# A two-layer attention and feed-forward kernel: the last 512 tokens in two halves of 256, with the closing work tile by tile

## Chip, cores, metric

One core of a Trainium2 chip. The metric is the device time of one execution in microseconds (us), as the median of several runs. A profile of one further execution gives the *span*, from the first to the last instruction; it lies 1.7 to 2.0 us under the time of that same execution.

## The reference, cut to what matters

```python
def _A_ref(x, wqkv, wo):          # 2048 tokens, width 512, 32 heads of 16
    qkv = (x @ wqkv) ...          # split into q, k, v by head
    scores = jnp.einsum("bhqd,bhkd->bhqk", q, k) * scale
    p = _softmax(scores, axis=-1)
    o = jnp.einsum("bhqk,bhkd->bhqd", p, v)
    return o.reshape(B, S, D) @ wo
def _B_ref(x, w1, b1, w2, b2):    # feed-forward, hidden width 1376
    h = _gelu(jnp.einsum("bsd,df->bsf", _layernorm(x), w1) + b1)
    return jnp.einsum("bsf,fd->bsd", h, w2) + b2

x = x + _A_ref(_layernorm(x), ...);  x = x + _B_ref(_layernorm(x), ...)
x = x + _A_ref(_layernorm(x), ...);  x = x + _B_ref(_layernorm(x), ...)
```

Every token attends to all 2048, so layers 1 and 3 (the attentions) each need 32 x 2048 x 2048 exponentials.

## The kernel before

The program is made by a list scheduler in Python: jobs hand it tasks with a modelled duration and a priority, and it fixes the order of instructions on each engine. That order is then the program; on the chip each engine runs its list and waits on semaphores. In modelled gaps of TensorE it puts *fillers*, multiplications by zeros that are meant to keep the clock up.

Attention goes block of 512 queries by block, and in each block head group by head group (8 groups of 4 heads). A *score tile* is 128 keys of one head by 512 queries. Four heads lie on four 32-row strips of TensorE, so tiles of different heads run at once. ScalarE exponentiates two or three tiles in one instruction; some tiles go to VectorE, which computes the exponential by a polynomial. Values are then accumulated in one PSUM bank, `ACCB`:

```python
ops.append(I(lambda e, ...: e.matmul(self.ps[:, b, :], lhsT=self.KT[32*hp:32*hp+32, hg, kb*128:(kb+1)*128],
             rhs=self.QT[32*hp:32*hp+32, q, :], start=True, stop=True, tile_position=(32*hp, 0)), ...))
yield Task("pe", 0.0, ops)
... e.activation(out=self.PT[:, pt:pt+n, :], in_=self.ps[:, b0:b0+n, :], func=ACTF.Exp, scale=EXPS)
```

When value matmuls are issued is decided in `try_pv`; the last line matters below:

```python
for it in near:                       # ready tiles of the current head group
    hp = sg["tiles"][it[1]][1]
    if hp not in seen:                # at most one tile for each strip
        seen.add(hp); pick.append(it)
        if len(pick) == 4: break
left = sg["n"] - sg["sub"]
if len(pick) < 4 and len(near) < min(left, 5):
    return                            # wait for more
```

At the end of a head group (`job_segend`) VectorE transposes the accumulator, divides and transposes back. When all 8 groups of a block are done, its projection, norm and feed-forward follow (`job_post`, `job_ffn`), beside the next block's scores. Those of the very last block have nothing beside them:

```python
def job_post(self, L, qc):
    yield ("keys", [("ot", L, qc, hg) for hg in range(8)])       # all head groups
    for i, tt in enumerate(tiles): ...                           # 4 projections, one after the other
    yield from self.ln_group(tiles, slot, ...)                   # statistics of all 4
    for i, tt in enumerate(tiles): S_.spawn(self.job_yt(...))    # scale, transpose by DMA
    yield ("keys", [("yt", L, tt) for tt in tiles])
    S_.spawn(self.job_ffn_tail(L, qc) if tail else self.job_ffn(L, qc), pr)
```

## Time and profile before

| | us |
|---|---|
| time, median of 4 runs (range) | 1851.19 (1846.91 to 1852.32) |
| span in the profile | 1851.3 |
| ScalarE / TensorE / VectorE busy | 1737.9 / 1723.7 / 1590.1 |
| last exponential ends at | 1804.67 |
| tail after it | 46.63 |

TensorE's busy time includes 519 us of fillers, so it is not a bound. The prediction shows the main lines. One more view is needed, the waits that end ScalarE's idle time in the last block. I give the last block one measure throughout: **U**, from the start of the accumulator transpose that ends the 72nd head group (the last group of the block before; 1587.22) to the end of the last exponential. U is 217.45 us. The *waits* view of the kernel before over that window (engine and tile, what it waited for, us in total, times, longest):

```profile
ACT PT L973 <- PE ps L967: 5.7, 11, 0.8
```

Four of the 11 waits are of 0.80 to 0.82 us (a fifth, of 0.78, is only 0.55 and 0.49 in runs c and f, whose scores have the same order). This is one of the four, in the *timeline* (start, duration, engine, line, tiles, number; in brackets the idle time ahead and what ended it):

```profile
1700.28 1.26 PE L905 MATMUL ps<-wqkv,zw 128*128 128x256 bf16 x10
1701.47 0.51 PE L1099 MATMUL ps<-PT,V 128*17 128x512 bf16 x4
1701.92 0.60 PE L967 MATMUL ps<-QT,KT 32*128 32x512 bf16 x6
1702.38 2.37 ACT L973 ACTIVATE PT<-ps 128x1024 bf16<-128x1024 f32 x2 [0.82 <-PE ps L967]
```

Ten fillers (the scheduler had foreseen a hole), then four value matmuls, then six score tiles at once: two groups of scores stood behind a full probability buffer. ScalarE, the bound, had nothing to do for 0.82 us. That the buffer was full is read from the scheduler, not from the trace (see the experiments).

### The profile page before, as it was taken

Reading aid. Unit: us, or ns where it says so; the run is one execution under the profiler, and the core shown is the slowest. Engines: PE = TensorE matmul, PEld = TensorE weight load, DVE = VectorE, ACT = ScalarE, POOL = GpSimd, SP = SyncE. Lnnn points to the kernel's source line nnn. Section 1 sums busy time; section 2 is a strip of 40 time slices with the busy share of each in tenths; the row PEclk is TensorE's granted clock in tenths of the full one; section 3 lists DMA queues with packets and bytes.
Section 4 is the critical chain, followed back from the end, with each engine's and each line's share of the span. In section 5 each row is a group of like instructions: output and inputs, shape, how many; then the busy total and the mean of one; then the engine's idle time right before and its main releaser. Section 6 shows DMA issues by size and latency. Waiting matters only on the chain.

```text
span 1851.3 us, 32298 instructions
## 1 busy us (share of the span) xinstructions
PE 1723.7 (93%) x13057; PEld 664.7 (36%) x13057; DVE 1590.1 (86%) x2469; ACT 1737.9 (94%) x1539; POOL 171.1 (9%) x324
## 2 busy tenths in 40 slices
PE   6989899999999999999999999999999999999997
PEld 2223333333333333333333333333333333333344
DVE  6789999988898999979987999878899789987972
ACT  4989999999999999999999999999999999999991
POOL 4122221100100110002000023100000000000000
PEclk9999999999999999999999999999999999999999
DMA  6551000100100200014310110000000000010001
GB/s 157 97 116 32 24 21 12 33 12 24 56 18 4 55 27 7 15 27 101 50 31 7 29 44 21 15 12 13 7 7 18 15 7 7 7 15 15 1 1 24
DMA packets 147226, 54.80 MB, mean 30 GB/s; under 512 B 131879, under 2 KB 140936, under 8 KB 147080
## 3 DMA queue, kind: packets, MB, share of 16 engines
q1 hardware_dynamic: 147080, 52.72, 12.8%
q8 instruction: 107, 1.75, 0.4%
q14 instruction: 39, 0.32, 0.1%
HBM read 8.69 MB, written 15.30 MB: 13 GB/s over the span
## 4 chain that ended last, share of the span: by engine, by line
ACT 53%; PE 36%; DVE 6%; DMA 2%; issue 1%; POOL 1%; SPq 0%; POOLq 0%; DVEq 0%
ACT PT L973 50%; PE ps L967 11%; PE ps L1099 7%; PE ps L905 5%; PE ps L1216 4%; PE ps L742 4%; PE ps L1250 3%; PE ps L1184 3%; ACT h L1243 2%; DMA xnT<-xn 1%; DVE dt L984 1%; DMA yT<-xn 1%; DVE de L1054 1%; DVE de L1051 1%; ACT L973 0%
## 5 line engine op out<-in xcount | busy, mean ns | idle before, releaser
L973 ACT ACTIVATE PT<-ps 128x1024 bf16<-128x1024 f32 (+1 forms) x1466 | 1665.0, 1289 | 59.8 <-PE ps L967 55.7
L967 PE MATMUL ps<-QT,KT 32*128 32x512 bf16 x4096 | 599.9, 382 | 85.8 <-ACT PT L973 61.3
L905 PE MATMUL ps<-wqkv,zw 128*128 128x256 bf16 x3508 | 518.8, 275 | 0.0
L1099 PE MATMUL ps<-PT,V 128*17 128x512 bf16 x3633 | 436.5, 384 | 3.6 <-DVE accT L1127 3.2
L984 DVE TENSOR_SCALAR dt<-ps 128x512 int32<-128x512 f32 x463 | 317.5, 686 | 136.1 <-PE ps L967 132.9
L905 PEld LDWEIGHTS ps<-wqkv,zw 128*128 128x128 bf16 x3508 | 289.7, 98 | 208.2 <-issue 176.2
L967 PEld LDWEIGHTS ps<-QT,KT 32*128 32x128 bf16 x4096 | 163.8, 91 | 499.5 <-issue 297.8
L1051 DVE SCALAR_TENSOR_TENSOR de<-dt 128x1024 bf16<-128x1024 uint16 (+1 forms) x244 | 283.8, 1164 | 2.2
L1054 DVE SCALAR_TENSOR_TENSOR de<-dt,dv 128x1024 uint16<-128x1024 int32 (+1 forms) x244 | 283.0, 1161 | 1.9
L1099 PEld LDWEIGHTS ps<-PT,V 128*17 128x17 bf16 x3633 | 105.2, 87 | 240.0 <-issue 204.9
L1053 DVE TENSOR_TENSOR dv<-de,dv 128x1024 f16<-128x1024 bf16 (+1 forms) x244 | 160.3, 658 | 2.1
L1052 DVE TENSOR_SCALAR dv<-dt 128x1024 bf16<-128x1024 uint16 (+1 forms) x244 | 161.0, 661 | 0.0
L1099 PE MATMUL ps<-de,V 128*17 128x512 bf16 x463 | 138.8, 384 | 2.1 <-DVE accT L1127 1.2
L678 POOL TENSOR_SCALAR rs<-mv 128x4 f32<-128x4 f32 (+1 forms) x19 | 10.0, 527 | 1070.5 <-DVE mv L671 1070.2
L1216 PE MATMUL ps<-yT,w 128*128 128x512 bf16 (+1 forms) x352 | 98.3, 392 | 8.0 <-DMA yT<-xn 6.9
L742 PE MATMUL ps<-wqkv,xnT 128*128 128x512 bf16 x336 | 95.4, 391 | 8.8 <-DMA xnT<-xn 8.0
L1250 PE MATMUL ps<-w,h 128*128 128x512 bf16 x280 | 74.8, 382 | 0.6 <-DVE xres L1252 0.3
L1127 DVE STREAM_TRANSPOSE accT<-ps 128x512 f32<-128x512 f32 x80 | 57.0, 712 | 16.1 <-PE ps L1099 14.4
L1184 PE MATMUL ps<-wo,OT 128*128 128x512 bf16 x256 | 69.2, 382 | 0.2
L1236 DVE TENSOR_SCALAR h<-ps,b1c 128x512 f32<-128x512 f32 (+1 forms) x77 | 56.8, 737 | 6.3 <-PE ps L1216 5.9
L1099 PEld LDWEIGHTS ps<-de,V 128*17 128x17 bf16 x463 | 31.5, 87 | 40.0 <-issue 31.3
L1216 PEld LDWEIGHTS ps<-yT,w 128*128 128x128 bf16 (+1 forms) x352 | 27.6, 101 | 50.8 <-issue 25.7
(123 smaller groups left out, 773.9 us busy)
## 6 DMA issues: line engine op xcount, KB each, us to landing
q_scr<-qk SPq DMA_DIRECT2D x22, 256.0 KB, 2.0
k_scr<-qk SPq DMA_DIRECT2D x12, 256.0 KB, 2.0
q_scr<-h SPq DMA_DIRECT2D x10, 256.0 KB, 2.1
out_dram<-xres SPq DMA_DIRECT2D x16, 128.0 KB, 1.7
v_scr<-vst SPq DMA_DIRECT2D x12, 136.0 KB, 1.9
V<-v_scr SPq DMA_DIRECT2D x8, 204.0 KB, 5.0
wqkv<-in_A_wqkv_dram SPq DMA_DIRECT2D x3, 512.0 KB, 5.0
w<-in_B_w_dram SPq DMA_DIRECT2D x4, 344.0 KB, 5.3
```

The source lines that it names most:

```text
L742: yield Task("pe", prio, [I(lambda e, c=c: e.matmul(self.ps[:, b, :], lhsT=xnT[:, c, :], rhs=self.wqkv[:, c, which * 512:which * 512 + 512 ...
L905: P.op("pe", lambda e: e.matmul(self.ps[:, b, 0:w], lhsT=self.zw[:, :], rhs=rhs, start=st, stop=st, skip_group_check=True), [("zw",), R], ...
L967: ops.append(I(lambda e, hp=hp, hg=hg, kb=kb, q=q, b=b: e.matmul(self.ps[:, b, :], lhsT=self.KT[32 * hp:32 * hp + 32, hg, kb * 128:(kb + 1 ...
L973: S_.submit(Task("act", 1e-5 * gi, [I(lambda e, pt=pt, n=n, b0=b0: e.activation(out=self.PT[:, pt:pt + n, :], in_=self.ps[:, b0:b0 + n, :] ...
L984: S_.submit(Task("dve", 0.0, [I(lambda e, ds=ds, w=w: e.tensor_scalar(out=self.dt32[:, ds, w * 512:(w + 1) * 512], in0=self.ps[:, DLANE, : ...
L1051: yield Task("dve", pr(), [I(lambda e: e.scalar_tensor_tensor(out=E, in0=lo, scalar=65536.0, in1=lo, op0=ALU.subtract, op1=ALU.mult), RT, ...
L1052: yield Task("dve", pr(), [I(lambda e: e.tensor_scalar(out=v, in0=lo, scalar1=CUB_B * sc / 65536.0, scalar2=CUB_A * sc, op0=ALU.mult, op1= ...
L1053: yield Task("dve", pr(), [I(lambda e: e.tensor_tensor(out=D, in0=E, in1=v, op=ALU.mult), [("de", es), ("dv", s)], [("dv", s)], 0.12 + 0.5 ...
L1054: yield Task("dve", pr(), [I(lambda e: e.scalar_tensor_tensor(out=Pb, in0=t32, scalar=2.0 ** -9, in1=D, op0=ALU.mult, op1=ALU.subtract), R ...
L1099: ops.append(I(lambda e, hp=hp, hg=hg, kb=kb, ap=ap, first=first: e.matmul(self.ps[32 * hp:32 * hp + 17, ACCB, :], lhsT=self.V[:, hg, kb, ...
L1216: yield Task("pe", pr, [I(lambda e, c=c: e.matmul(self.ps[0:M, b, :], lhsT=self.w1[:, c, fc * 128:fc * 128 + M], rhs=self.yT[:, c, :], sta ...
L1250: yield Task("pe", pr, [I(lambda e, fc=fc, i=i, b=b: e.matmul(self.ps[:, b, :], lhsT=self.gt(fc, i), rhs=self.w2[:, fc, :], start=(fc == 0 ...
```

## The change

The intent: less work behind the last exponential. The last block becomes two blocks of 256 queries, so that only 256 tokens are left for the tail. A score tile of the half-width blocks holds two key blocks side by side, 512 columns again, so exponentials keep their shape. The tail's projection is accumulated head group by head group as they end, each tile has its own statistics, and TensorE transposes in place of the DMA. In the tail's feed-forward, a second-layer matmul now waits for the gelu of its own chunk of the hidden width, not for that of four chunks. Nothing else changes: the other blocks keep widths and modelled durations.

```diff
+        four = [tuple(range(4 * c, 4 * c + 4)) for c in range(self.NC)]
+        self.units = {1: four, 3: four[:3] + [four[3][:2], four[3][2:]]}
...
+            g = 512 // sg["W"]
+            sg["tiles"] = [(sg["kbs"][k:k + g], hp) for k in range(0, len(sg["kbs"]), g) for hp in range(4)]
...
+    def score(self, sg, j, b):
+        return [I(lambda e, ...: e.matmul(self.ps[:, b, i * W:(i + 1) * W], lhsT=self.KT[..., kb * 128:(kb + 1) * 128], rhs=self.QT[..., q, 0:W], ...)) for i, kb in enumerate(kbs)]
...   (value matmuls likewise; accumulator, transposes and scalings W wide)
-    def job_ffn_tail(self, L, qc):
+    def job_tail(self, L, qc):
+        yield ("keys", [("post",) + self.prev(L, qc)] + [("ot", L, qc, hg) for hg in range(7)])
+        for i, tt in enumerate(tiles):
+            S_.spawn(self.tail_tile(L, qc, tt, slot, i, left), 1.0 + 0.1 * i)
         yield ("keys", [("scores_done",)])
+        yield Task("act", pr, [... activation(out=self.kmx[:, 2:3], ..., func=ACTF.Gelu_apprx_tanh) ...])   # loads the table early
...   (feed-forward as before, W wide)
+    def tail_tile(self, L, qc, tt, slot, i, left):
+        pr = 0.9
+        b = yield ("get", "mb")
+        for h0 in range(8):
+            if h0 == 7:
+                yield ("keys", [("ot", L, qc, 7)])
+            yield Task("pe", pr, [... matmul(self.ps[:, b, :], lhsT=self.OT[:, h0, i*128:(i+1)*128], rhs=self.wo[:, h0, :], start=(h0 == 0), stop=(h0 == 7)) ...])
+        ...  # add, bn_stats, bn_aggr, variance and power on GpSimd, scale
+        yield Task("pe", pr, [... transpose(...) for k in range(4)])
+        yield Task("dve", pr, [... tensor_copy(out=self.yT[:, :, i*128:(i+1)*128], in_=...) ...])
```

## The prediction

> **What bounds the kernel now.** I read the page first: the sliced busy row of ScalarE (ACT) and the chain of waits.
>
> ```profile
> ACT  4989999999999999999999999999999999999991
> ...
> ACT 53%; PE 36%; DVE 6%; DMA 2%; issue 1%; POOL 1%; SPq 0%; POOLq 0%; DVEq 0%
> ACT PT L973 50%; PE ps L967 11%; PE ps L1099 7%; PE ps L905 5%; PE ps L1216 4%; PE ps L742 4%; PE ps L1250 3%; PE ps L1184 3%; ACT h L1243 2%; DMA xnT<-xn 1%; DVE dt L984 1%; DMA yT<-xn 1%; DVE de L1054 1%; DVE de L1051 1%; ACT L973 0%
> ```
>
> ScalarE is full from the third slice to the last but one, with the exponentials of L973 carrying half of the chain. Only the last slice (46 us) has it nearly empty. So there are two regimes: a long stretch where the time is ScalarE's, and a tail. The last exponential ends at 1804.67 in the timeline (1803.65 + 1.02), and the span is 1851.3, so the tail is 46.63 us. I cut the last 250 us into windows, two for the last 512 tokens' scores and two for the tail.
>
> ```profile
> core 0: us, PE busy (x) PEld busy (x) DVE busy (x) ACT busy (x) POOL busy (x), PEclk, DMA share, GB/s
> 1604.00:1704.00 100.00, 94.55 (x707) 35.99 (x707) 81.73 (x124) 95.56 (x81) 2.40 (x2) 1.00 0.08 16
> 1704.00:1804.67 100.67, 93.88 (x785) 40.33 (x783) 83.93 (x118) 99.05 (x88) 0.00 (x0) 1.00 0.00 1
> ...
> 1804.67:1825.37 20.70, 14.89 (x106) 9.75 (x104) 9.41 (x20) 1.28 (x2) 1.20 (x2) 0.97 0.15 27
> 1825.37:1851.30 25.93, 21.93 (x88) 9.06 (x88) 2.49 (x4) 7.55 (x11) 0.00 (x0) 0.89 0.06 21
> ```
>
> In the second window ScalarE idles 1.6 us of 100.67. The first also holds the projection, norm and feed-forward of the previous 512 tokens; ScalarE idles 4.4 us there. In the tail it works 8.84 us of 46.63. The chain says what the tail waits for:
>
> ```profile
> 1804.59 0.53 PE ps L1099 x5
> ...
> 1807.39 5.62 PE ps L1184 x26
> ...
> 1816.75 0.19 DVE mv L671
> ...
> 1818.78 2.45 DMA yT<-xn
> ...
> 1821.75 0.87 SPq L1209
> ...
> 1822.72 2.52 DMA yT<-xn
> ...
> 1825.37 7.60 PE ps L1216 x22
> 1832.97 4.32 PE ps L1282 x20
> 1837.29 3.45 PE ps L1216 x16
> 1840.74 3.45 PE ps L1282 x16
> ```
>
> Four 128-token tiles go through the projection one after another, all four are normalised, two rounds of transposing DMAs follow, and then come 88 matmuls of 512 columns. The first of those 88 are slow: 22 in 7.60 us, later 16 in 3.45 (0.216 each). Ahead of them TensorE had waited 5.81 us.
>
> **What the Trainium skill says.** "TensorE: Matmul & The Clock Gate", section "Back-to-back issue gap", gives N/2.4 + 2.5 ns warm: 216 ns at 512 columns and an estimate of 109 at 256. The trace agrees: 3.45/16 = 0.216, and the 128x256 fillers of L905 come 0.11 us apart. Its section "What's actually happening" says an idle window of some 3.4 us halves the clock; here 5.81 us of idling was followed by matmuls 0.43 us apart. "Part 3: Packing small matmuls", section "The mechanism", says that a weight load overlaps matmuls in flight only where the row group differs. That would hurt score tiles built from two matmuls on one row strip. The trace does not show the harm: a group of four scores took 0.40 us, and another, where I read two tiles on one strip, took 0.59, just one more pass of 512 columns. "ScalarE: Activation LUTs", section "What ACT_TABLE_LOAD costs", gives 1283 ns per load; all loads here take 1283.
>
> **The change, part by part.** (a) *The first half's feed-forward moves under the scores of the second half.* ScalarE is the bound there, so its gelu is paid in full: two table loads 2 x 1.283 = 2.57; the 5120-column gelu takes 4.471, and with 2560 columns fewer at 0.833 ns it is 2.34; the 512-column one of 0.631 becomes 0.42. With gaps 5.4 us. Its VectorE work takes score tiles away from VectorE:
>
> ```profile
> 1604.00:1704.00 100.00, 17.20 (x25) 1.00 0.08 16
> 1704.00:1804.67 100.67, 20.54 (x30) 1.00 0.00 1
> ```
>
> These are the VectorE score loads (L984) in the same two windows: 25 tiles beside a whole block's post-processing, 30 without. Half a block: 2.5 tiles, at 0.427 us of ScalarE each, 1.1 us. ScalarE's waits for scores were 4.0 against 1.6 us, so half of the difference, 1.2 us, comes as waiting.
>
> (b) *16 head-group ends instead of 8.* One end on VectorE is 0.712 + 0.246 + 0.420 + 0.699 = 2.08 us. VectorE's slope is 1.0 ns a column (1217 ns for 1024 columns, 700 for 512), so at half width 0.45 + 0.25 + 0.29 + 0.44 = 1.43. 16 x 1.43 - 8 x 2.08 = 6.3, plus about 1.5 for 8 more query scalings: 7.8 us. A VectorE score tile costs 0.686 + (1217 + 1215 + 688 + 683)/2 ns = 2.59 us, so 3.0 tiles go to ScalarE: 1.3 us. Beside the last 8 ends, once the post-processing is over, the timeline shows two ScalarE stalls of 0.82 us (at 1702 and 1737); 8 more ends, 1.6 us.
>
> (c) *Score and value matmuls of the unit double in number at half width.* Exponentials keep count and shape, since a 512-column tile now holds two key blocks. On TensorE the extra cost lies in slack. In 1704 to 1804.67 there are 245 score and 253 value matmuls; the fillers alone take 42.84 us. Even 25 ns for each of about 500 added matmuls is 12 us of that. Charge: 0.
>
> Sum for ScalarE: 5.4 + 1.1 + 1.2 + 1.3 + 1.6 = 10.6 us. The last exponential would end at 1815.3.
>
> (d) *The tail for 256 tokens*, counted from the last exponential, T. The end of the last head group starts 0.49 after T as now, 1.43 of work and 0.12 of gaps: T + 2.04. Seven of eight head groups are already accumulated for tile 0 and can be for tile 1, so 0.49 later (as now) its add starts, T + 2.53. Two adds and two statistics at about 0.66 (VectorE takes the other tile while one waits), then the aggregation 0.18: T + 5.4. GpSimd: 0.19 and then 0.583 for one column (four columns took 1.01), with 0.2 of gaps: T + 6.3. The second tile's power follows at T + 7.0, its scaling 0.42, four TensorE transposes about 0.4 with latency, a PSUM copy of 0.53 (the one such copy in the trace) with latency: first feed-forward matmul at about T + 8.6, against 20.70 now. The idle stretches of TensorE are short and filled, so I count it warm. Then 44 x 0.11 + 22 x 0.216 = 9.6 us of matmuls and 0.5 for the last gelu not covered: T + 18.7. The last two matmuls start 0.43 before that; 0.41 later the first add, two adds 1.29, the store 2.12 (1849.18 to 1851.30 now): T + 22.1. Now it is 46.63: 24.5 us less.
>
> Sum: 1851.3 + 10.6 - 24.5 = 1837.4 of span; the timed median lies 0.5 above the span, so about **1838 us**, 0.75% faster. Up to some 1590 us nothing changes: the other blocks keep their widths and modelled durations, hence their order.
>
> **Rivals.** *TensorE becomes the pace-setter of the last unit.* Each group of scores or values then has two passes with weight loads between; if each of the some 165 exponentials of those two windows waited 0.1 us more, 17 us would go and the time would be near 1855. For it: the skill's sentence on row groups, and that a wait for scores already ends most of ScalarE's idling. Against: the 0.59 us group above and the 42.84 us of fillers. *The tail starts cold.* If transposes and fillers do not keep the clock up, the 44 narrow matmuls take up to 0.213 each, 4.5 us more: about 1842. Against: clock 0.97 up to 1825.37, lost after idling of 5.8 us, which the new chain does not have in one piece. *The exposed work hides better than I charge*: if VectorE's added work falls in its idle 17% and no stalls come, only the 5.4 us remain and the time is 1833. *The tail is limited by chains between engines*: tile 1's steps may not interleave with tile 0's, and the order is fixed by a model of durations; 3 us either way.
>
> **Range and chances.** The cost side may be 6 to 18 us, the gain 20 to 26. Not all extremes meet, so 1830 to 1847. Faster by over 2% needs less than about 1815.5, that is 36 us; the tail cannot give that as 22 us of it must stay. Slower by over 2% needs some 60 us lost in a 210 us unit, only under the first rival at three times its size. So 0.02, 0.96 and 0.02.
>
> **What would show it.** In the changed kernel: the last exponential near 1815 (1810 says the hidden work was nearly free, over 1822 that TensorE or the ends hold ScalarE up); one gelu of 2.3 us with two table loads among the last unit's exponentials; the last unit's exponential count about 5 higher; ScalarE's waits for scores in the last 100 us near 4 us. After it: first feed-forward matmul 8 to 10 us after the last exponential, no transposing DMA there, matmuls 0.11 us apart, 22 to 24 us from last exponential to end. The prediction is wrong if score groups make ScalarE wait regularly, or if the tail keeps 30 us.

## More of the kernel before

(The execution profiled before took 1853.09 us, longer than the four timed.)

The probabilities have five buffers (three of three tiles, two of two), and a buffer comes free when all its tiles have been multiplied with the values.

## The result, and the profile after

| | before | after |
|---|---|---|
| time, median of 4 runs (range), us | 1851.19 (1846.91 to 1852.32) | 1829.3 (1827.47 to 1831.81) |
| span of the profile | 1851.3 | 1827.5 |
| U (last block up to the last exponential) | 217.45 | 219.34 |
| tail after the last exponential | 46.63 | 23.19 |

A ratio here is the mean time of one kernel's fast runs over that of the other's of the same rounds, so not quite the ratio of the medians: 0.9887, with a 95% interval of 0.9867 to 0.9907. That is within 2%. The 1838 predicted is 8.7 us too slow; the median lies just outside the range's low end of 1830, though 0.9887 times the 1851.81 known when I predicted is 1830.9, just inside.

U and the tail together changed by +1.9 - 23.4 = -21.5 us. The spans differ by 23.8; the other 2.3 us lie ahead of U, where both run the same code (the 72nd group ends at 1587.22 before, 1584.97 after). Up to there, executions differ: in the twelve profiles that share the order up to there (all but i and j), the 72nd group ended between 1580.9 (e2, granted clock 0.998 over the run) and 1595.5 (c, granted clock 0.990). U repeats far better where the order of the scores is the same: 217.45 and 217.32 (c); 219.34, 219.11 (d) and 219.21 (g). So for differences of a few us I compare U and the tail, not times.

The page after, slices and chain shares, for comparison with the first lines of the prediction:

```profile
ACT  5989999999999999999999999999999999999996
...
ACT 58%; PE 34%; DVE 5%; DMA 2%; issue 1%; POOL 1%; SPq 0%; DVEq 0%; POOLq 0%
```

The last slice of ScalarE went from 1 to 6 tenths. The windows after, up to the last exponential in two parts, then up to the first feed-forward matmul, then to the end (columns as in the prediction):

```profile
1585.00:1690.00 105.00, 96.53 (x1170) 39.05 (x1168) 91.99 (x156) 103.20 (x88) 2.08 (x2) 1.00 0.06 14
1690.00:1804.31 114.31, 103.91 (x1328) 43.59 (x1327) 98.36 (x162) 113.98 (x100) 2.18 (x2) 1.00 0.05 11
1804.31:1814.32 10.01, 7.55 (x63) 4.91 (x64) 5.76 (x14) 1.49 (x2) 1.49 (x4) 1.00 0.01 2
1814.32:1827.50 13.18, 9.90 (x66) 6.25 (x66) 1.29 (x2) 4.95 (x11) 0.00 (x0) 1.00 0.06 20
```

ScalarE idles 0.33 us of 114.31 in the second window. The tail's two parts are 10.01 and 13.18 us, against 20.70 and 25.93, and the clock is full. The moved gelu stands among the exponentials (timeline of ScalarE after):

```profile
1681.42 67.74 ACT L979 ACTIVATE PT<-ps 128x1536 bf16<-128x1536 f32 x59 [0.20 <-PE ps L1005]
1749.18 1.28 ACT L1263 ACT_TABLE_LOAD   x1
1750.47 2.34 ACT L1263 ACTIVATE h<-h 128x2560 bf16<-128x2560 f32 x1
1752.84 0.42 ACT L1264 ACTIVATE g<-h 96x256 bf16<-96x256 f32 x1
1753.27 1.28 ACT L979 ACT_TABLE_LOAD   x1
1754.57 49.74 ACT L979 ACTIVATE PT<-ps 128x1024 bf16<-128x1024 f32 x44
```

That is 5.32 us of new work, as predicted, and yet U grew by only 1.9. The *windows* view over U, before and then after:

```profile
1587.22:1804.67 217.45, 204.31 (x1607) 81.48 (x1606) 181.80 (x263) 211.21 (x183) 2.40 (x2) 1.00 0.04 8
1584.97:1804.31 219.34, 200.47 (x2497) 82.64 (x2496) 190.38 (x318) 217.21 (x188) 4.26 (x4) 1.00 0.06 12
```

ScalarE's busy time in U rose from 211.21 to 217.21, by 6.0: the gelu, and one more exponential instruction, of two tiles, as VectorE took 58 score tiles in place of 60. Its idle time fell from 6.24 to 2.13, by 4.1. The waits view after, over U:

```profile
ACT PT L979 <- PE ps L1005: 1.5, 6, 0.4
```

From 11 waits and 5.7 us to 6 waits and 1.5 us; none of 0.8 is left. The saving is in the waits that I had expected to grow; in the last 100 us, where I had expected near 4 us of waits, that view is empty. The tail after, in the chain (start, duration, what):

```profile
1804.36 1.68 PE ps L1334 x7
1806.05 0.55 PE ps L1113 x10
...
1808.17 0.40 PE ps L1334
1808.60 1.29 DVE xres L1336 x2
...
1813.84 0.44 DVE yT L1351
1814.32 1.49 PE ps L1235 x12
1815.81 1.29 PE ps L1310 x6
```

No DMA is left between the projection (L1334) and the feed-forward (L1235). But seven projection matmuls stand ahead of the last ten value matmuls (L1113), on which everything else waits.

### The profile page after: what moved, and what is told of

The parts are those of the page before. It is cut to its first block, busy times and chain, and to the rows that moved or that the text cites. A ratio compares the mean times of both kernels' runs of the same rounds, so it can differ in the third digit from the quotient of the medians.

```text
span 1827.5 us, 34039 instructions
## 1 busy us (share of the span) xinstructions
PE 1702.4 (93%) x13894; PEld 658.9 (36%) x13894; DVE 1593.4 (87%) x2516; ACT 1741.9 (95%) x1545; POOL 172.9 (9%) x328
## 4 chain that ended last, share of the span: by engine, by line
ACT 58%; PE 34%; DVE 5%; DMA 2%; issue 1%; POOL 1%; SPq 0%; DVEq 0%; POOLq 0%
ACT PT L979 54%; PE ps L1005 10%; PE ps L1113 6%; PE ps L914 4%; PE ps L750 4%; PE ps L1235 3%; PE ps L1270 3%; PE ps L1203 3%; ACT h L1263 2%; DMA xnT<-xn 1%; DVE dt L990 1%; ACT L979 1%; ACT L1263 1%; DVE de L1064 1%; DVE de L1067 0%
## 5 line engine op out<-in xcount | busy, mean ns | idle before, releaser
L1005 PE MATMUL ps<-QT,KT 32*128 32x512 bf16 (+1 forms) x4608 | 605.3, 358 | 92.6 <-ACT PT L979 69.4
L914 PE MATMUL ps<-wqkv,zw 128*128 128x256 bf16 x3269 | 488.3, 276 | 0.0
L1113 PE MATMUL ps<-PT,V 128*17 128x512 bf16 (+1 forms) x4086 | 437.7, 361 | 3.6 <-DVE accT L1143 3.2
L914 PEld LDWEIGHTS ps<-wqkv,zw 128*128 128x128 bf16 x3269 | 269.4, 98 | 196.2 <-issue 166.0
L1113 PEld LDWEIGHTS ps<-PT,V 128*17 128x17 bf16 x4086 | 108.9, 87 | 238.1 <-issue 204.1
L1113 PE MATMUL ps<-de,V 128*17 128x512 bf16 (+1 forms) x522 | 137.3, 359 | 1.9 <-DVE accT L1143 0.9
L686 POOL TENSOR_SCALAR rs<-mv 128x4 f32<-128x4 f32 (+2 forms) x19 | 10.9, 572 | 967.1 <-DVE mv L679 966.8
L1235 PE MATMUL ps<-yT,w 128*128 128x512 bf16 (+3 forms) x396 | 97.1, 359 | 1.7 <-DMA yT<-xn 0.7
L1143 DVE STREAM_TRANSPOSE accT<-ps 128x512 f32<-128x512 f32 (+1 forms) x88 | 58.3, 662 | 15.8 <-PE ps L1113 13.9
L1257 DVE TENSOR_SCALAR h<-ps,b1c 128x512 f32<-128x512 f32 (+2 forms) x88 | 61.8, 702 | 7.8 <-PE ps L1235 7.4
L1183 DVE STREAM_TRANSPOSE OT<-ob 128x512 bf16<-128x512 bf16 (+1 forms) x72 | 46.0, 640 | 0.0
L1113 PEld LDWEIGHTS ps<-de,V 128*17 128x17 bf16 x522 | 32.2, 87 | 38.2 <-issue 29.5
```

Source lines behind the costliest of these rows:

```text
L914: P.op("pe", lambda e: e.matmul(self.ps[:, b, 0:w], lhsT=self.zw[:, :], rhs=rhs, start=st, stop=st, skip_group_check=True), [("zw",), R], ...
L1005: return [I(lambda e, kb=kb, i=i: e.matmul(self.ps[:, b, i * W:(i + 1) * W], lhsT=self.KT[32 * hp:32 * hp + 32, hg, kb * 128:(kb + 1) * 12 ...
L1113: ops.append((i, I(lambda e, hp=hp, hg=hg, kb=kb, ap=ap[:, i * W:(i + 1) * W], first=first and i == 0, W=W: e.matmul(self.ps[32 * hp:32 * ...
L1235: yield Task("pe", pr, [I(lambda e, c=c: e.matmul(self.ps[0:M, b, off:off + W], lhsT=self.w1[:, c, fc * 128:fc * 128 + M], rhs=self.yT[:, ...
```

## The experiments

Questions: (1) Why did the 5.3 us of moved work cost so little? Theory S: the kernel before had lost 4 us of its last block to stalls that are accidents of one instruction order; the change reshuffled that order, and its saving there is not owed to the halves. Rival W: half-width blocks are kinder to ScalarE by their nature. (2) Is doubling the matmuls free? (3) Is the moved gelu paid in full? (4) What are halves and tile-by-tile style worth in the tail, and why does it start 1.4 us later than predicted?

For (1), S can be made concrete. The builder was made to print where it holds a score group: at each of the stalls, in its own modelled times, the scores wait 2.3 us for a two-tile probability buffer although some tiles are ready, because `try_pv` wants four tiles of different strips or five tiles in all.

This print is not a run. Repeated on the fourteen kernels, it gives holds of 2.3 us in the last block as follows: four in the kernel before, in c and in f, two in the kernel before with edit k, none in the others. That is in each trace the number of waits of 0.80 to 0.93 us. When the rule refuses for the last time in such a hold, three or four tiles are ready, but on two or three strips only.

**a. The rule relaxed, last block only, in the kernel before; b. the same in the changed kernel.**

```diff
-            if len(pick) < 4 and len(near) < min(left, 5):
+            if len(pick) < 4 and len(near) < min(left, 4 if sg["L"] == 3 and sg["qc"] >= 3 else 5):
```

> The kernel before, with one rule changed in its last 512 tokens only: value matmuls are issued once 4 score tiles are ready (5 before), even when fewer than 4 fit different strips. Call U the time from the accumulator's transpose that ends the last head group of the block before (1587.22 us before, 1584.97 after) to the end of the last exponential: 217.45 us before, 219.34 after. Theory S (stalls): the kernel before lost about 4 us of U to score waits that are accidents of its instruction order (0.8 us each), so halving looked nearly free. Then U falls to about 213.5 here, the 0.8 us waits go, the tail stays 46.6, and the time is 3 to 4 us lower (0.998). Rival W (width): half-width blocks are kinder to ScalarE by themselves; then this rule leaves the waits and U within 1 us of 217.5.

> The changed kernel with the same rule in its two last halves. Theory S: it has no such waits to lose, so U stays at 219.3 within 1.5 us, and the halving costs 5 to 8 us of U against the run a_before_relaxed instead of 1.9. Rival W: U stays too, but the difference from a_before_relaxed stays near 2 us. Tail 23.2 in both.

Measured, with 3 rounds: a has U 212.49 and tail 45.96, b U 220.97 and tail 23.01. The waits view over U, a and then b:

```profile
ACT PT L973 <- PE ps L967: 2.4, 8, 0.4
```

```profile
ACT PT L979 <- PE ps L1005: 1.1, 5, 0.3
```

The 0.8 us waits of the kernel before are gone, and U fell by 5.0, of which 3.6 us are ScalarE's idle time and 1.4 us its busy time. In b U rose by 1.6, just past what I had allowed. Between the two kernels with this rule, halving costs 8.5 us of U, not 1.9. VectorE took 62 tiles in a and 54 in b. The timed runs do not show the gain of a: its ratio is 1.0 (0.9982 to 1.0019), which excludes the 0.997 that U and the tail promise. Its four runs were granted 0.992 to 0.993 of the clock, those of the kernel before 0.993 to 0.997, so the loss may lie ahead of the last block, in code that both share; this is not shown. b has 0.9907 (0.9873 to 0.994).

**k. Another disturbance of the order, in both kernels.**

```diff
-        if len(sg["todo"]) < DTAIL:          # DTAIL = 16
+        if len(sg["todo"]) < (14 if sg["L"] == 3 and sg["qc"] >= 3 else DTAIL):
```

> A second, unlike disturbance of the order of the last 512 tokens in the kernel before: VectorE may take score tiles until 14 are left in a head group (16 before). If the waits in that block are accidents of one order, some of the four 0.8 us waits go or move: U 214 to 216 (217.45 before). If they belong to 512-wide blocks, U 217 or more.

> The same disturbance in the changed kernel. U 219.5 to 221 (219.34 in the changed kernel), so the halves cost 4 to 7 us of U against k_before_tail14, between 1.9 (the two kernels) and 8.5 (the relaxed pair). If the halves are kind to ScalarE by themselves: below 3.

Measured, one look each: U 213.39 in the kernel before with this edit, 221.08 in the changed one. Both moved the way S said, each a little past its range; halving costs 7.7 us here, where I had said 4 to 7. Two of the 0.8 us waits remained in the first, and 2.7 us of waits in all.

**j. The relaxed rule in the whole kernel before.** Same line as in a, `min(left, 4)` everywhere.

> The kernel before with the relaxed rule (4 for 5) in the whole kernel: control for the fastest candidate. Waits of 0.8 us go in all blocks. If the gains add, it lies 4 to 8 us under the kernel before (ratio 0.996 to 0.998), and the halves with the changed tail are then worth some 20 us more. U 212.5 to 214, tail 46. If the rule is worth nothing without halves (rival), ratio 1.0 and U 217.

Measured, 5 rounds: 1835.03 us (1833.36 to 1839.97), ratio 0.9929 (0.9912 to 0.9946), about twice the gain expected. U is 211.34, under its range, and the tail 46.17. All of ScalarE's waits for scores fell from 55.7 us in 95 waits to 36.6 in 69. With run i below, the third pair for question 1: U 219.01 against 211.34, so 7.7 us.

**f. Matmuls doubled, nothing else.** The kernel before, with the same order on all engines; in the last block each group of score or value matmuls is issued as all left halves, then all right halves:

```diff
+                if isinstance(g, tuple):                 # a group of the last block
+                    for op in ops: op.fn(eng, 0, 256)
                 for op in ops:
-                    ins = op.fn(eng)
+                    ins = op.fn(eng, 256, 512) if isinstance(g, tuple) else op.fn(eng)
```

> The kernel before, in the same order on every engine, but in its last 512 tokens each score and value matmul of 512 columns is issued as two of 256 (all left halves of a group, then all right halves). If doubling is free, as predicted, U is 217.4 within 1.0 and the waits of ScalarE for scores from 1583 us on stay near 4.6 to 5.7 us in total. Rival (TensorE's two passes delay each score group by 0.1 us): U 225 or more, many waits. Tail 46.6.

Measured, one look: U 217.11, waits 5.4 us, tail 45.7. Free, as predicted. Only where ScalarE was stalled anyway does it show: the four long waits are 0.91 to 0.93 us in place of 0.80 to 0.82. A score group of three tiles takes no longer as six narrow matmuls; this line from the timeline of the changed kernel is one:

```profile
1800.52 0.39 PE L1005 MATMUL ps<-QT,KT 32*128 32x256 bf16 x6
```

**e, e2. The moved gelu without its table loads.** The first half's gelu becomes an exponential (a wrong result; relative error 0.03), first in the old order, then with the shorter duration told to the scheduler.

```diff
-  func=ACTF.Gelu_apprx_tanh), HR, HR, 1.5 + 0.427 * nf * W / 512)
+  func=ACTF.Exp if L == 3 and qc == 3 else ACTF.Gelu_apprx_tanh), HR, HR, ...)      # e2 also: 0.2 + 0.427 * nf * W / 512 there
```

> The changed kernel with the first half's gelu replaced by an exponential, which needs no table change (a wrong result on purpose; same instruction order). If the moved gelu is paid in full on ScalarE, its two table loads of 1.283 us disappear from U: 219.34 - 2.57 = 216.8 (within 0.7), tail 23.2. Rival (ScalarE has slack there, so the moved work was hidden): U stays 219.3.

> As e_no_table (wrong result on purpose), and the order is built with the shorter duration, so no instruction is queued ahead for a longer gelu. If ScalarE pays the two table loads in full, U is 219.34 - 2.57 = 216.8 within 0.6. If what e_no_table showed (218.6) is the true worth because the moved work lies in slack, U stays near 218.6.

Measured, one look each: U 218.63 in e and 218.02 in e2; neither theory's number. Of 2.57 us taken away, 0.7 and 1.3 us came through, although ScalarE's busy time fell by 2.6 and 2.7. The waits for scores rose from 1.5 us to 3.5 and 3.0: right after the shorter gelu, new waits of 1.62 and 1.06 us appear. In e, whose order was made for the longer gelu, TensorE had a run of 29 fillers (3.34 us) and six feed-forward matmuls ahead of the next scores. In e2 the fillers are gone, but the six matmuls ran at half pace, with a granted clock of 0.60 from 1747 to 1751:

```profile
1747.67 2.64 PE L1270 MATMUL ps<-w,h 128*128 128x512 bf16 x6 [1.86 <-ACT g L1264]
```

At 0.216 us each, six take 1.3 us. The scores behind them would then have come in time, and U would lie near 217.0 (an estimate from this line and the 1.06 us wait; not run), which is the number for a gelu paid in full. So the table loads are on ScalarE's path, and what did not come through are waits of the altered kernels; that the gelu is paid in full is likely, not shown.

**c. Only the tile-by-tile tail, on 512 tokens; d. only the halves, closed in the old style.**

```diff
c:  -  3: four[:3] + [four[3][:2], four[3][2:]]
    +  3: four
d:  -  if L == 3 and qc == len(self.units[L]) - 1: yield from self.job_tail(L, qc); return
    +  tail = L == 3 and qc == len(self.units[L]) - 1     # then as before: 4 -> 2 projections, one batch of statistics,
                                                           # DMA transposes, then the feed-forward of job_tail
```

> Only the tile-by-tile closing work, on all of the last 512 tokens, no halves. U should stay 217.5 (same order of the scores). The tail then shows what the new tail style is worth without fewer tokens: first feed-forward matmul some 15 us after the last exponential (20.7 before), then 44 + 44 matmuls of 512 columns warm, 19 us, and the same end: tail 39 to 41 us (46.6 before), time about 0.9965 of before. If the halves are what saves (rival), the tail stays above 44.

> Only the two halves; the last half is closed in the old style (all projections, all norms, transposing DMAs, then the feed-forward). U as in the changed kernel, 219.3 within 1. Tail: two projections, one statistics batch and one or two rounds of transposing DMA, so first feed-forward matmul 12 to 15 us after the last exponential (10.0 in the changed kernel), a clock that may fall, then 10 us: tail 27 to 31 us (23.2 in the changed kernel). Time about 0.991 to 0.993 of before. If the tile-by-tile style is worth nothing here (rival), 23 to 24.

Measured: c has U 217.32 and tail 40.14; d U 219.11 and tail 26.76, a hair under its range, with the first feed-forward matmul 12.2 us after the last exponential and the clock warm. So of the 23.4 us that the tail lost, the halves alone give 19.9 and the style alone 6.5; together they overlap, and the style adds 3.6 on top of halves. (In c 20 projections, 4.48 us, stand ahead of the last value matmuls, so 6.5 is what the style gives in this order; compare g.) The ratios agree within their intervals: 0.9984 (0.996 to 1.0007) for c, 0.9918 (0.9892 to 0.9943) for d. In d the transposing DMA is still in the chain:

```profile
1819.36 0.91 SPq L1226
...
1820.31 2.52 DMA yT<-xn
```

**g. Value matmuls first.** The projections of head groups 0 to 6 in the tail get less urgency (1.05) than value matmuls (1.0).

```diff
-            yield Task("pe", pr, [... matmul ... lhsT=self.OT[:, hg, ...] ...])
+            yield Task("pe", pr if h0 == 7 else 1.05, [...])
```

> The changed kernel, with the closing projection of head groups 0 to 6 given less urgency than value matmuls. In the changed kernel the second tile's seven projections (1804.36 to 1805.98) stand ahead of the last 10 value matmuls. If they are what made the tail start 1.4 us later than predicted, the first feed-forward matmul comes 8.5 to 8.9 us after the last exponential (10.0 now), the tail is 21.6 to 22.0 (23.2 now), U 219.3. Rival (the last value matmuls wait for something else, the probabilities say): 9.8 or more and 23.

Measured: U 219.21, first feed-forward matmul 8.30 us after the last exponential, tail 21.47: better than expected by a little. Time 1828.81 (1825.39 to 1830.19), ratio 0.9868 (0.985 to 0.9885). The chain of g shows the two groups swapped:

```profile
1806.83 0.65 PE ps L1113 x10
1807.48 1.62 PE ps L1334 x7
...
1815.23 1.49 PE ps L1235 x12
```

**i. Run g with the relaxed rule everywhere**, a candidate for the fastest.

> The same with the relaxed rule for value matmuls (4 in place of 5) in the whole kernel: a candidate for the fastest. Stalls elsewhere go, about 3 us before the last 512 tokens, tail 21.8: time 1822 to 1827, ratio to before 0.984 to 0.987. If the rule only moves waits about (rival): ratio 0.988 to 0.990, as g.

Measured, 4 runs timed: 1821.93 us (1821.66 to 1824.24), ratio 0.984 (0.9825 to 0.9854), correct. U 219.01, tail 21.53. It is 1.6% faster than before, against 1.1% for the change; the two were timed in different rounds, each against the kernel before.

The last block in the profiles of question 1 (c, d, e, e2, f and g stand above; e, e2, f and k have granted clocks, 0.993 to 0.998):

| kernel | U | waits for scores in U (us, times) | score tiles on VectorE | tail |
|---|---|---|---|---|
| before | 217.45 | 5.7, 11 | 60 | 46.63 |
| before, relaxed in the last block (a) | 212.49 | 2.4, 8 | 62 | 45.96 |
| before, 14 for 16 (k) | 213.39 | 2.7, 5 | 62 | 45.44 |
| before, relaxed everywhere (j) | 211.34 | 1.2, 5 | 62 | 46.17 |
| changed | 219.34 | 1.5, 6 | 58 | 23.19 |
| changed, relaxed in the last block (b) | 220.97 | 1.1, 5 | 54 | 23.01 |
| changed, 14 for 16 (k) | 221.08 | 1.6, 6 | 55 | 22.52 |
| changed, values first, relaxed everywhere (i) | 219.01 | 0.7, 2 | 55 | 21.53 |

In i and j two score tiles fewer are left at the start of U (505 in place of 507), some 0.9 us of ScalarE; their difference is not touched by this.

## Why the prediction was right or wrong

**What bounds the kernel: right.** ScalarE sets the time up to the last exponential, the tail's chain after it; the sum stayed within 2%. (The 0.5 us from span to median compared two different executions.)

**The tail (step d): right in its parts.** 24.5 us less predicted, 23.4 measured. The first feed-forward matmul came 10.0 us after the last exponential, not 8.6; I had left unsaid what the second tile's seven projections would do to the last value matmuls. Run g, which only reorders those, starts at 8.30. From the first feed-forward matmul to the end I had 22.1 - 8.6 = 13.5 us; measured 13.18.

**The cost on ScalarE: mis-sized, 10.6 predicted, 1.9 measured.** Term by term:

- "With gaps 5.4 us" for the moved gelu: 5.32 us of instructions, so right as work. Runs e and e2 leave open whether the path pays all of it.
- "2.5 tiles" and "3.0 tiles go to ScalarE", 2.4 us: 2 tiles in this pair, 0.85 us (one more exponential, where I had said about five); 7 or 8 tiles, 3.0 to 3.4 us, in the three disturbed pairs.
- "half of the difference, 1.2 us, comes as waiting" and "8 more ends, 1.6 us": this is the step that failed, in sign. The waits fell by 4.2 us. I took the 0.8 us stalls as a price for each head-group end and multiplied it. They come from the rule for value matmuls and the order of tiles, as the count of 2.3 us holds shows: a 512-wide last block in three other orders has waits of 1.2 to 2.7 us in place of 5.7, while the half-width block with its gelu intact never has more than 1.6.
- Doubled matmuls, "Charge: 0": right (f).

So the halves cost about 8 us of U when the block before is free of most such stalls (8.5, 7.7 and 7.7 in three pairs, of which a and j share one rule), which is near the 10.6 predicted without the waits (7.8). The delivered pair shows 5.8 to 6.6 us less than that, and only about half of the difference is stalls. ScalarE's idle time fell by 4.1 us in the delivered pair and by 0.6 to 1.1 in the others: 3.0 to 3.5 us. The other 2.3 to 3.5 us are ScalarE's busy time, which rose by 6.0 us in the delivered pair and by 8.3 to 9.5 in the others, because VectorE gave up two score tiles there and seven or eight here. Both come with the order; which count of tiles is usual for halves is not shown.

Theory S stands: most of the saving in waits is not owed to the halves. W is not quite excluded: in every pair the half-width kernel still has fewer waits, by 0.5 to 1.3 us. Why the new order has none of the 2.3 us holds was not followed.

**The rivals.** TensorE as pace-setter: refuted by f. A cold tail: refuted, clock 1.00 in both windows of the tail. "The exposed work hides better", 1833: nearest to what came, but for another reason, since VectorE did not take up the work for nothing.

## What to carry to other kernels

A stall seen in a statically ordered program may be an accident of that order and not a price of the feature beside it; before multiplying it by a count, change the order in some unlike way and see whether it stays. Compare a change on a base freed of such stalls too, or the luck of the order is booked as the change's merit: here the base alone gained 0.7% from one number in a rule. Cutting the last block makes the unshared tail shorter almost in proportion (46.63 to 26.76 us for half the tokens, d), and costs its fixed parts (here a gelu with two table loads, and smaller shares for the helping engine) on the engine that bounds the rest.

## What the Trainium skill lacked or had wrong

- "ScalarE: Activation LUTs", section "What ACT_TABLE_LOAD costs": the load of 1283 ns agrees, but the drain of about 1380 ns that the page adds to each switch does not show. The exponentials end at 1749.16, the load starts at 1749.18, and the gelu at 1750.47; the switch costs 1.3 us. Without both loads (e), ScalarE was busy for 2.6 us less.
- "TensorE: Matmul & The Clock Gate", section "The mechanism" of Part 3: it says that weight loads overlap matmuls in flight only where the row group differs (though it also lets a load into a background buffer be pulled ahead). Six matmuls of 256 columns, in pairs on one strip, took 0.39 us from 1800.52 on, as long as three of 512, and all six weight loads were over by 1800.62, so the second load on each strip was hidden. Doubling about 1000 matmuls so (f) left U at 217.11 against 217.45.
- No page that I read gives the scatter in time between executions of one order: the same 72 head groups ended between 1580.9 and 1595.5 us in twelve profiles, at granted clocks of 0.998 and 0.990 over the run, which hides effects of 5 us from the timed runs.
